# A planned attention-plus-MLP kernel: new planner rules, longer stretches, and another string of rules

## The chip, the cores and the metric

The kernel runs on one core of a Trainium2 chip. The metric is the device time of one execution, in microseconds (us). A core has five engines with instruction streams of their own, which meet at semaphores: TensorE (PE in the profile; PEld is its weight loads), VectorE (DVE), ScalarE (ACT), GpSimd (POOL) and SyncE (SP), which issues transfers. TensorE writes into PSUM, eight banks of 128 partitions by 512 float32 columns. The other engines read PSUM and write to SBUF.

## What is computed

One block on a sequence of 2048 rows of width 640. The input is normalized; 32 heads of width 20 attend to one shared key and value head; a dense layer with silu (width 1728) runs beside them; all is added to the input.

```python
x = A_x
xn = _layernorm(x, axis=-1)
return x + _A_ref(xn, A_wq, A_wk, A_wv, A_wo) + _B_ref(xn, B_w1, B_w2)
# _A_ref
scores = jnp.einsum("bhqd,bkd->bhqk", q, k) * (Dh ** -0.5)
p = _softmax(scores, axis=-1)
o = jnp.einsum("bhqk,bkd->bhqd", p, v)
# _B_ref
h = _silu(jnp.einsum("bsd,df->bsf", x, w1))
out = jnp.einsum("bsf,fd->bsd", h, w2)
```

## The kernel before

**Tiles of scores.** The queries are cut into 4 chunks of 512 rows, the heads into 8 sets of 4. A group is one chunk with one set of heads: 32 groups. In each group there are 16 blocks of 128 keys and 4 heads, so 64 tiles of 128 keys by 512 queries, 2048 in all. Each tile is one matmul of contraction 32 (`s_mm`, L1078). Four heads sit in four row groups of the array, so up to four such matmuls run at once: a *score burst*.

**Two ways to the exponential.** A tile goes one of two ways.

- By ScalarE: two or three tiles in neighbouring banks are read by one `Exp` instruction (L1166) and written to a ring of 20 slots in SBUF. When the four heads of a key block are there, one *value pass* (four column matmuls, L1201, kind `p`) multiplies them by the values and adds into a PSUM bank of the group.
- By VectorE: four tiles of one key block are turned, one after the other (the first pass, L1409), into 16-bit integers that are the bits of a rough power of two. Two shifted copies of the four tiles are made by VectorE (L1453) or GpSimd (L1448), and three value passes (kind `pd`) use the three versions with fixed weights, so that the errors of the rough power cancel in the sum.

`claim` picks the key blocks that go by VectorE, `make_s_act` the tiles that go by ScalarE, as the planner comes to them. The division is thus an outcome of the planning.

**Other work of TensorE.** Projections of queries and the dense layer run as sets of four column matmuls (L447; some, cut by rows, ride in free row groups of score bursts: L454). They fill the time between score bursts. Changing between score bursts (row tiles) and the sets of column matmuls is called a turn here.

**Who sets the order.** All instruction streams are written by a planner on the host, before the program is built (`build`, class `Sched`). It keeps a clock for each engine with costs in nanoseconds for each operation, and takes, step by step, the operation that comes next on the engine that is furthest behind. On TensorE `step_pe` does this: it lists what could run, each with a kind (`s` score burst for ScalarE, `d` a tile for VectorE, `p` and `pd` the two kinds of value passes, `m` and `l` other matmuls, `r` a row piece of one), keeps those that are ready within 40 ns, and takes the first by a list of kinds. Which list depends on the array's mode and on how far the value passes lag behind the exponentials:

```python
        order = ["s", "m0"]
        if mode == "s":
            order += ["d", "r"]
            order += ["p", "pd", "m", "l"] if lag >= ru.lagmax else ["m", "pd", "p", "l"]
```

If nothing is ready for a while, `filler` puts in a matmul of zeros (L1725). The numbers that steer all this (`ru.lagmax`, `ru.open`, `ru.need` and so on) come from `BASE`. They are altered for stretches of planned time: a string `PLAN` holds one letter for each stretch of `PIECE` nanoseconds, and a letter names a set of changed numbers in `RULES`. Past the end of the string the letter is "a", which changes nothing.

```python
        if sc.t["pe"] >= piece * PIECE:
            ru.__dict__.update(BASE)
            ru.__dict__.update(RULES[rule(piece)])
            piece += 1
```

`emit` then turns the planned order into streams with semaphore waits. On the chip each engine follows its stream in order.

**The end.** When the last group's value passes are done, ScalarE copies the bank to SBUF (L1302), TensorE adds up the softmax denominators (L999), VectorE takes reciprocals (L1002), TensorE spreads them (L1017), VectorE multiplies (L1026), and the last projections (L447) are stored (L967, L984). The dense layer's last products, in sets of 320 columns, are put where the planner finds room.

Of the kernel before, what the change touches and what calls it, by code (L numbers as in the profile page):

```python
# [14 lines left out]
P = 128  # L15
D = 640
H = 32
# [64 lines left out]
POOL_J = (2,)  # L82
SWITCH = {"s": 97.0, "p": 98.0, "f": 98.0}
SPRIO = 0.5
PIECE = 10000.0
STEPS = 1
YC = (0, 0, 3, 3)
EARLY = 1
# [13 lines left out]
ACT_LN = (5, 7)  # L102
TRACT = (0, 1)

BASE = dict(uopen=4, umin=3, uleft=3, uwait=500.0, pace=-1.0, lagl=3, half=6, hold2=0, bnd=4, pj=6000.0, rows=0, rowmin=3, lagmax=6, lagp=0, lagj=6, openlag=5, late=-0.02, lead=0.01, leadmax=0.02, need=640.0, hold=300.0, dwant=600.0, slack=700.0, dnow=400.0, hungry=0.0, patience=0.0, keep=460.0, open=2, zcap=9, stay=0.0, homes=1, want=1, claim=6)
RULES = dict(a={}, b=dict(keep=0.0), c=dict(lagp=3), d=dict(lagp=5), e=dict(lagp=0), f=dict(patience=200.0), g=dict(dwant=0.0),
             h=dict(zcap=4), i=dict(zcap=3), j=dict(homes=0), k=dict(leadmax=-1.0, lead=-1.0), l=dict(lead=0.08, leadmax=0.1),
             m=dict(need=740.0), n=dict(hold=0.0), o=dict(stay=640.0), p=dict(open=1), q=dict(slack=560.0), r=dict(hungry=1000.0), s=dict(claim=9), t=dict(open=3), u=dict(claim=4), v=dict(want=2), w=dict(slack=850.0), x=dict(hold2=4), y=dict(bnd=0), z=dict(pj=-1e9), A=dict(rows=0), B=dict(rows=2, rowmin=2), C=dict(pj=2000.0), D=dict(openlag=3), E=dict(pj=8000.0), F=dict(hold2=3), G=dict(rows=1), H=dict(half=0), I=dict(half=3), J=dict(stay=560.0), K=dict(stay=720.0), P=dict(need=560.0), Q=dict(hold=120.0), L=dict(uopen=3), M=dict(uopen=4), N=dict(uopen=5), O=dict(uopen=0))
PLAN = "acbgxnoQpQJvpnaQodtxzpvEoQJBJoaodpJqQaDqJovpkBrnvxBxQJBfaaooHoatano"


def rule(n):
    return PLAN[n] if n < len(PLAN) else "a"
PACE = 1.0
# [214 lines left out]
def build(nc, A_x, A_wq, A_wk, A_wv, A_wo, B_x, B_w1, B_w2, out, stack):  # L329
    S = A_x.shape[1]  # L330
    F = B_w1.shape[1]
# [86 lines left out]
    R = {}  # L418
# [613 lines left out]

    ru = SimpleNamespace(**BASE)
    att = {"sgroup": 0, "pgroup": 0, "n": 0, "items": 0, "value": 0.0, "lead": 0.0}
# [327 lines left out]
    def dve_items():  # L1362

        busy = sc.pe_set[1] if sc.pe_set is not None and sc.t["pe"] <= sc.pe_set[2] + 1.0 else frozenset()
        pick = None
        if cur_job[0] is not None and cur_job[0].job.rest:
            need = {r for v in cur_job[0].job.rest.values() for r in v}
            if len(need - busy) == 1:
                pick = next(((st, j) for st in open_b for j in st["left"] if j not in busy and j not in need), None)
        if pick is None:  # L1370
            pick = next(((st, j) for st in open_b for j in st["left"] if j not in busy), None)
        if pick is None and len(open_b) < ru.open:
            c = claim()
            if c is not None:
                g, kt = c
                st = {"g": g, "kt": kt, "zi": z_slot(), "left": list(range(HG)), "p1": [], "pv": None, "jobs": {}}
                batches.append(st)
                z_last[st["zi"]] = st
                open_b.append(st)
                pick = next(((st, j) for j in st["left"] if j not in busy), None)  # L1380
        if pick is None and open_b:
            pick = open_b[0], open_b[0]["left"][0]
        if pick is None:
            return None
        st, i = pick
        if i not in st["jobs"]:
            st["jobs"][i] = dve_job(st, i)
        return st["jobs"][i]
# [431 lines left out]
    def xbank_est(mode):  # L1820
        return min(bank_at(b, mode) for b in xbanks())

    def dve_idle(t):
        for op in sc.pools["dve"]:
            e = sc.est(op)
            if e is not None and e < t:
                return False
        return True
# [13 lines left out]
    def step_pe():  # L1842
        t = sc.t["pe"]
        mode = sc.pe_mode
        rd = []
        late = None
        s_at = None
        for op, kind, what in pe_candidates():
            e = sc.est(op)
            if e is None:  # L1850
                continue
            if what[0] == "pv":
                if fresh_u():
                    e = max(e, xbank_est(op.mode))
                else:
                    e = max([e] + [o.fin + sc.way(o, op) for o in sc.hazards_of(sc.banks[ubank[what[1]]]) if o.eng != "pe"])
            if what[0] in ("new", "dj"):
                if what[0] == "dj" or (what[1][0].job.bank is None and what[1][0].job.fixed is None):
                    e = max(e, xbank_est(op.mode))
            if kind == "d" and not sc.joined(op) and not (sc.t["dve"] < t + ru.hungry and dve_idle(t + ru.hungry)):  # L1860
                continue
            if kind == "s":
                rest = sc.free.difference(op.run)
                if not pro and rest:
                    dj = dve_items()
                    if dj is not None:
                        for tb in sorted(bank_at(b, "s") for b in rest)[:ru.want]:
                            if e < tb <= act_until(att["n"]) - ru.slack:
                                e = tb
                s_at = e  # L1870
                if ru.keep and mode == "f" and cur_job[0] is not None and t + 250.0 < act_until(att["n"]) - ru.keep:
                    e = max(e, t + 240.0)
            if e <= t + 40:
                rd.append((kind, op, e, what))
            elif late is None or e < late[0]:
                late = (e, op, what)
        lag = lag_now()
# [4 lines that stand above are left out]
        elif mode == "p":  # L1882
            order += ["p", "pd", "m", "d", "l"] if lag >= (ru.lagj if cur_job[0] is not None else ru.lagl if att["lead"] < ru.pace else ru.lagp) else ["m", "pd", "p", "d", "l"]
        else:
            order += ["p", "m", "pd", "d", "l"] if lag >= ru.lagmax + 1 else ["m", "l", "pd", "p", "d"]
        if mode != "s" and sc.t["dve"] < t + ru.dnow and dve_idle(t + ru.dnow):
            order.remove("d")
            order.insert(2, "d")
        if ru.stay and mode != "s" and not pro and t + 230.0 < act_until(att["n"]) - ru.stay:
            order.remove("s")  # L1890
            order.insert(len(order) - 1, "s")
        if all(not u for u in unclaimed) and not make_s_act():
            order = ["p", "pd", "d", "r", "m0", "m", "l", "s"]
        order += ["z", "x"]
        if ru.bnd and att["pgroup"] < NGR and pv_left[att["pgroup"]] <= ru.bnd and not pro:
            order = [k for k in order if k not in ("m", "l")] + [k for k in order if k in ("m", "l")]
        best = None
        for kind, op, e, what in rd:
            if kind not in order:
                continue  # L1900
            k = order.index(kind)
            if best is None or k < best[0]:
                best = (k, op, e, what)
        if best is not None:
            op = best[1]
            if op.mode != mode and s_at is not None and s_at - t < WAITS and op.mode != "s":
                return s_at, None, None
            return best[2], op, best[3]
        gap = 999.0 if late is None else late[0] - t
        if gap > (FILLGAP if mode != "p" or not att["n"] else FILLGAP2) and (streamed() < FILL or not att["n"]) and (pro or misc or make_s_act()):  # L1910
            op = filler(gap)
            e = sc.est(op) if op is not None else None
            if e is not None and e <= t + 40:
                return e, op, ("fill", None)
        if late is None:
            return None
        return late[0], late[1], late[2]

    def fresh_u():
        return att["pgroup"] < NGR and att["pgroup"] not in ubank  # L1920
# [63 lines left out]
    while not finished():  # L1984
# [3 lines that stand above are left out]
# [186 lines left out]
```

## Time and profile before

| | |
|---|---|
| median of 3 runs | 689.98 us (689.96 to 690.01) |
| profiled execution | 690.16 us |
| its span, first to last instruction | 688.3 us |
| TensorE busy | 675.7 us (98%) |
| ScalarE busy | 666.4 us (97%) |
| VectorE busy | 591.3 us (86%) |
| GpSimd busy | 581.7 us (85%) |
| granted TensorE clock | 1.0 |

A row of a group names the line, the engine, the operation, what is written and read, the shape and the count; behind the bar stand the busy time, the mean length of one and the idle time ahead of them, with what ended it. A row of the order in time has the start, the length, and the same names; several equal instructions in a row are one line. Matmuls overlap: the length of one is from issue to its modelled end, so the distance between starts tells what one costs its engine. The same holds for ScalarE, whose records overlap a little.

### The profile page before, as it was taken

To read this page: it belongs to the slowest core of one execution; us is meant where nothing else is said; L and a number is where in the kernel's file an instruction comes from. 1 tells how busy PE (TensorE), PEld (TensorE's weight loads), DVE (VectorE), ACT (ScalarE), POOL (GpSimd) and SP (SyncE) were. 2 spreads that over 40 slices of the span, in tenths; PEclk is the share of its full clock that TensorE was granted. 3 is DMA by queue.
4 is the path that set the end of the run, shared out by engine and by line. 5 is a ranking of instruction groups with operands and counts; after the bars stand their busy time and mean duration, and the time that the engine had idled before them with its cause. 6 is when DMAs were issued, how large, how long until landed. Compare 5 with 4: busy or idle time off the path is not lost.

```text
span 688.3 us, 22511 instructions
## 1 busy us (share of the span) xinstructions
PE 675.7 (98%) x9821; PEld 232.2 (34%) x9821; DVE 591.3 (86%) x1017; ACT 666.4 (97%) x728; POOL 581.7 (85%) x349
## 2 busy tenths in 40 slices
PE   8999999999999999999999999999999999999998
PEld 6432222222333333322323333332233333333345
DVE  7899988999989878798898897889999898987953
ACT  6999999999999999999999999999999999999992
POOL 6658899898988998899898889888889987879990
PEclk9999999999999999999999999999999999999999
DMA  8643220222221222422022222132222221223201
GB/s 226 190 160 42 19 23 14 35 34 25 23 29 12 32 38 29 72 36 30 9 22 30 29 31 33 26 37 61 31 22 20 21 27 23 32 20 70 23 7 41
DMA packets 34241, 28.97 MB, mean 42 GB/s; under 512 B 15486, under 2 KB 29662, under 8 KB 34142
## 3 DMA queue, kind: packets, MB, share of 16 engines
q1 hardware_dynamic: 33854, 27.20, 25.8%
q8 instruction: 77, 1.26, 0.8%
q10 hardware_dynamic: 288, 0.33, 0.1%
q14 instruction: 22, 0.18, 0.1%
HBM read 11.09 MB, written 2.62 MB: 20 GB/s over the span
## 4 chain that ended last, share of the span: by engine, by line
ACT 52%; PE 42%; DVE 3%; POOL 1%; DMA 0%; issue 0%; DVEq 0%; ACTq 0%
ACT sbt L1166 48%; PE psall L1201 14%; PE psall L1078 14%; PE psall L447 13%; ACT sbt L773 3%; DVE sbt L1409 2%; POOL sbt L1448 1%; PE psall L595 1%; PE psall L621 1%; DVE sbt L1453 0%; DMA sbt<-in_A_x_dram 0%; PE psall L999 0%; PE psall L1017 0%; ACT sbt L554 0%; DVE sbt L565 0%
## 5 line engine op out<-in xcount | busy, mean ns | idle before, releaser
L1166 ACT ACTIVATE sbt<-psall 128x1024 bf16<-128x1024 f32 (+1 forms) x656 | 640.0, 1138 | 3.2 <-PE psall L1078 3.0
L1448 POOL TENSOR_SCALAR sbt<-sbt 128x2048 int16<-128x2048 int16 x273 | 518.6, 1900 | 72.5 <-PE psall L1201 15.3
L1409 DVE TENSOR_SCALAR sbt<-psall 128x512 int16<-128x512 f32 x676 | 440.1, 685 | 63.1 <-PE psall L1078 58.0
L1078 PE MATMUL psall<-sbt 32*128 32x512 bf16 x2048 | 268.3, 384 | 3.3 <-ACT sbt L1166 2.0
L1201 PE MATMUL psall<-sbt 128*32 128x512 bf16 x3400 | 264.7, 384 | 1.9 <-POOL sbt L1448 0.6
L447 PE MATMUL psall<-sbt 128*32 128x320 bf16 (+2 forms) x3772 | 225.9, 332 | 2.1 <-DVE sbt L776 0.7
L1078 PEld LDWEIGHTS psall<-sbt 32*128 32x128 bf16 x2048 | 71.8, 91 | 236.9 <-ACT sbt L1166 174.1
L447 PEld LDWEIGHTS psall<-sbt 128*32 128x32 bf16 x3772 | 80.4, 95 | 85.5 <-issue 45.4
L1201 PEld LDWEIGHTS psall<-sbt 128*32 128x32 bf16 x3400 | 68.8, 94 | 115.5 <-issue 71.9
L1453 DVE TENSOR_SCALAR sbt<-sbt 128x2048 int16<-128x2048 int16 x65 | 47.6, 750 | 0.0
L860 POOL TENSOR_TENSOR sbt<-sbt 128x512 bf16<-128x512 f32 x30 | 38.3, 1277 | 4.9 <-DVE sbt L1453 2.7
L776 DVE SCALAR_TENSOR_TENSOR sbt<-sbt,psall 128x512 bf16<-128x512 bf16 x52 | 35.5, 682 | 3.8 <-ACT sbt L773 1.8
L773 ACT ACTIVATE sbt<-psall 128x512 bf16<-128x512 f32 x52 | 34.9, 671 | 0.2 <-PE psall L447 0.2
L454 PE MATMUL psall<-sbt 32*128 32x320 bf16 (+1 forms) x78 | 24.4, 313 | 0.0
L1250 DVE COPY sbt<-psall 128x512 f32<-128x512 f32 x31 | 21.2, 683 | 0.9 <-PE psall L1201 0.8
L919 DVE SCALAR_TENSOR_TENSOR sbt<-psall,sbt 128x320 f32<-128x320 f32 x8 | 3.9, 491 | 12.2 <-PE psall L447 7.0
L903 DVE SCALAR_TENSOR_TENSOR sbt<-psall,sbt 128x320 bf16<-128x320 f32 x24 | 11.6, 482 | 3.1 <-PE psall L447 1.7
L693 DVE TENSOR_SCALAR sbt<-psall 128x512 bf16<-128x512 f32 x20 | 13.5, 676 | 0.0
L572 POOL TENSOR_TENSOR sbt<-sbt 128x2 f32<-128x2 f32 x8 | 5.7, 710 | 8.5 <-DVE sbt L570 8.2
L1725 PE MATMUL psall<-sbt 128*32 128x256 bf16 (+1 forms) x188 | 11.1, 375 | 1.2 <-DVE sbt L487 1.2
L585 POOL TENSOR_SCALAR sbt<-sbt 128x640 bf16<-128x640 bf16 x12 | 10.4, 878 | 1.5 <-DVE sbt L577 1.5
L563 DVE BATCH_NORM_STATS2 sbt<-sbt 128x6 f32<-128x320 bf16 x14 | 6.6, 472 | 2.0 <-DMA sbt<-in_A_x_dram 2.0
(64 smaller groups left out, 118.3 us busy)
## 6 DMA issues: line engine op xcount, KB each, us to landing
sbt<-sbt SPq DMA_DIRECT2D x120, 64.0 KB, 3.8
sbt<-in_A_x_dram SPq DMA_DIRECT2D x28, 160.0 KB, 3.9
sbt<-sbt SPq DMA_DIRECT2D x213, 20.0 KB
out_dram<-sbt SPq DMA_DIRECT2D x14, 160.0 KB, 2.2
sbt<-in_B_w_dram SPq DMA_DIRECT2D x1, 2160.0 KB, 11.5
sbt<-in_B_w_dram SPq DMA_DIRECT2D x1, 2080.0 KB, 8.2
sbt<-sbt SPq DMA_DIRECT2D x75, 8.0 KB
sbt<-in_A_wq_dram SPq DMA_DIRECT2D x1, 800.0 KB, 6.7
```

The source lines that it names most:

```text
L447: ins = pe.matmul(ps[j * SLOT:(j + 1) * SLOT, b * BANK + off:b * BANK + off + n], w[:, j * SLOT:(j + 1) * SLOT], x, start=start, stop=stop ...
L454: return pe.matmul(ps[0:w.shape[-1], b * BANK:b * BANK + n], w[k], x[k], start=start, stop=stop, tile_position=(r * SLOT, 0))
L773: t = Op("act", lambda a: a.activation(t_buf[0:rows, ts, :], bk(job.bank, 0, QW, rows=rows), AF.Tanh, scale=0.5), t_act(512), ACT_END, pre ...
L776: u = Op("dve", lambda v: v.scalar_tensor_tensor(out=hT[par][0:rows, fk, :], in0=t_buf[0:rows, ts, :], scalar=1.0, in1=bk(job.bank, 0, QW, ...
L860: nm = pool(lambda e: e.tensor_tensor(oU[:, us, :], U_sb[:, us, :], Rrep, ALU.mult), 1356.0, POOL_END, pre=[uc] + lc + pack_op.get(divmod( ...
L1078: return pe.matmul(bk(b), kT_rep[i * SLOT:(i + 1) * SLOT, kt * P:(kt + 1) * P], qT[i * SLOT:(i + 1) * SLOT, g % NQ, :], start=True, stop=T ...
L1166: return a.activation(Ebuf[:, es * QW:es * QW + w], ps[:, buf[0] * BANK:buf[0] * BANK + w], AF.Exp, scale=ESCALE)
L1201: ins = pe.matmul(ps[i * SLOT:(i + 1) * SLOT, ub * BANK:ub * BANK + QW], lhsT, rhs, start=(first and k < HG), stop=(last and k >= len(lst) ...
L1250: return v.tensor_copy(U_sb[:, us, :], bk(ub))
L1409: p1 = Op("dve", lambda v: v.tensor_scalar(z16[:, i * QW:(i + 1) * QW], bk(job.bank), ZBIAS, 0.0, ALU.add, ALU.max), t_dve(QW) + 2.0, DVE_ ...
L1448: op = pool(lambda v, t=t, j=j, zin=zin: v.tensor_scalar(t.bitcast(I16), zin, float(SHIFT[j]), 1.0, ALU.add, ALU.mult), POOL_SHIFT, POOL_E ...
L1453: op = dve(lambda v, t=t, j=j, zin=zin: v.tensor_scalar_add(t.bitcast(I16), zin, float(SHIFT[j])), t_dve(N, 4), prio=SPRIO - 0.01 * j, **args)
```

## The change

- `BASE` gets a new number `pdf`, 0 unless a rule sets it. In `step_pe`, when it is 1, the kind `pd` (value passes of VectorE's tiles) is put just ahead of `p` (those of ScalarE's); when it is 2, into second place of the list.
- `RULES` gets three letters: R (`pdf` 1), S (`pdf` 2), T (`pdf` 1 and `lagp` 3).
- `PIECE` goes from 10 to 16 us of planned time.
- `PLAN` is another string, of 42 letters in place of 67. R is at three places of it (the thirteenth, fourteenth and twenty-third stretch), S and T at none.

The rest of the text of the kernel is the same. What TensorE, and behind it the other engines, do in which order follows from the string.

```diff
-PIECE = 10000.0
+PIECE = 16000.0
...
-BASE = dict(uopen=4, umin=3,
+BASE = dict(pdf=0, uopen=4, umin=3,
...
+ R=dict(pdf=1), S=dict(pdf=2), T=dict(pdf=1, lagp=3))
-PLAN = "acbgxnoQpQJvpnaQodtxzpvEoQJBJoaodpJqQaDqJovpkBrnvxBxQJBfaaooHoatano"
+PLAN = "apQdxxjnrnvQRRnomBoamCRqhJPJahEzraJBnBBGQF"
...
         if all(not u for u in unclaimed) and not make_s_act():
             order = ["p", "pd", "d", "r", "m0", "m", "l", "s"]
+        if ru.pdf and "pd" in order:
+            order.remove("pd")
+            order.insert(order.index("p") if ru.pdf == 1 else 1, "pd")
         order += ["z", "x"]
```

More of the change, by code (lines that the diff above doesn't have):

```diff
@@ L103 @@
 TRACT = (0, 1)
-BASE = dict(uopen=4, umin=3, uleft=3, uwait=500.0, pace=-1.0, lagl=3, half=6, hold2=0, bnd=4, pj=6000.0, rows=0, rowmin=3, lagmax=6, lagp=0, lagj=6, openlag=5, late=-0.02, lead=0.01, leadmax=0.02, need=640.0, hold=300.0, dwant=600.0, slack=700.0, dnow=400.0, hungry=0.0, patience=0.0, keep=460.0, open=2, zcap=9, stay=0.0, homes=1, want=1, claim=6)
+BASE = dict(pdf=0, uopen=4, umin=3, uleft=3, uwait=500.0, pace=-1.0, lagl=3, half=6, hold2=0, bnd=4, pj=6000.0, rows=0, rowmin=3, lagmax=6, lagp=0, lagj=6, openlag=5, late=-0.02, lead=0.01, leadmax=0.02, need=640.0, hold=300.0, dwant=600.0, slack=700.0, dnow=400.0, hungry=0.0, patience=0.0, keep=460.0, open=2, zcap=9, stay=0.0, homes=1, want=1, claim=6)
 RULES = dict(a={}, b=dict(keep=0.0), c=dict(lagp=3), d=dict(lagp=5), e=dict(lagp=0), f=dict(patience=200.0), g=dict(dwant=0.0),
              h=dict(zcap=4), i=dict(zcap=3), j=dict(homes=0), k=dict(leadmax=-1.0, lead=-1.0), l=dict(lead=0.08, leadmax=0.1),
-             m=dict(need=740.0), n=dict(hold=0.0), o=dict(stay=640.0), p=dict(open=1), q=dict(slack=560.0), r=dict(hungry=1000.0), s=dict(claim=9), t=dict(open=3), u=dict(claim=4), v=dict(want=2), w=dict(slack=850.0), x=dict(hold2=4), y=dict(bnd=0), z=dict(pj=-1e9), A=dict(rows=0), B=dict(rows=2, rowmin=2), C=dict(pj=2000.0), D=dict(openlag=3), E=dict(pj=8000.0), F=dict(hold2=3), G=dict(rows=1), H=dict(half=0), I=dict(half=3), J=dict(stay=560.0), K=dict(stay=720.0), P=dict(need=560.0), Q=dict(hold=120.0), L=dict(uopen=3), M=dict(uopen=4), N=dict(uopen=5), O=dict(uopen=0))
-PLAN = "acbgxnoQpQJvpnaQodtxzpvEoQJBJoaodpJqQaDqJovpkBrnvxBxQJBfaaooHoatano"
+             m=dict(need=740.0), n=dict(hold=0.0), o=dict(stay=640.0), p=dict(open=1), q=dict(slack=560.0), r=dict(hungry=1000.0), s=dict(claim=9), t=dict(open=3), u=dict(claim=4), v=dict(want=2), w=dict(slack=850.0), x=dict(hold2=4), y=dict(bnd=0), z=dict(pj=-1e9), A=dict(rows=0), B=dict(rows=2, rowmin=2), C=dict(pj=2000.0), D=dict(openlag=3), E=dict(pj=8000.0), F=dict(hold2=3), G=dict(rows=1), H=dict(half=0), I=dict(half=3), J=dict(stay=560.0), K=dict(stay=720.0), P=dict(need=560.0), Q=dict(hold=120.0), L=dict(uopen=3), M=dict(uopen=4), N=dict(uopen=5), O=dict(uopen=0), R=dict(pdf=1), S=dict(pdf=2), T=dict(pdf=1, lagp=3))
+PLAN = "apQdxxjnrnvQRRnomBoamCRqhJPJahEzraJBnBBGQF"
 def rule(n):
```

## The prediction

> **What bounds the kernel now.** I read the page's busy shares, then the groups by shape, then the order in time of ScalarE, then its end.
>
> ```profile
> span 688.3 us, 22511 instructions
> PE 675.7 (98%) x9821; PEld 232.2 (34%) x9821; DVE 591.3 (86%) x1017; ACT 666.4 (97%) x728; POOL 581.7 (85%) x349
> ACT 52%; PE 42%; DVE 3%; POOL 1%; DMA 0%; issue 0%; DVEq 0%; ACTq 0%
> ```
> ```profile
> L1166 ACT ACTIVATE sbt<-psall 128x1024 bf16<-128x1024 f32 x594 | 563.5, 1100 | 2.6 <-PE psall L1078 2.5
> L1166 ACT ACTIVATE sbt<-psall 128x1536 bf16<-128x1536 f32 x61 | 89.7, 1512 | 0.6 <-PE psall L1078 0.6
> L1166 ACT ACTIVATE sbt<-psall 128x512 bf16<-128x512 f32 x1 | 0.7, 700 | 0.0
> L773 ACT ACTIVATE sbt<-psall 128x512 bf16<-128x512 f32 x52 | 34.9, 671 | 0.2 <-PE psall L447 0.2
> ```
> ```profile
> 13.64 1.92 ACT L1166 ACTIVATE sbt<-psall 128x1024 bf16<-128x1024 f32 x2
> ...
> 22.62 7.44 ACT L1166 ACTIVATE sbt<-psall 128x1024 bf16<-128x1024 f32 x8 [0.48 <-PE psall L1078]
> 29.87 0.68 ACT L631 ACTIVATE sbt<-psall 128x512 bf16<-128x512 f32 x1
> ...
> 48.97 0.77 ACT L773 ACTIVATE sbt<-psall 128x512 bf16<-128x512 f32 x1
> 49.44 5.82 ACT L1166 ACTIVATE sbt<-psall 128x1024 bf16<-128x1024 f32 x6
> ...
> 671.73 1.54 ACT L1166 ACTIVATE sbt<-psall 128x1536 bf16<-128x1536 f32 x1
> 673.07 1.54 ACT L1166 ACTIVATE sbt<-psall 128x1536 bf16<-128x1536 f32 x1
> 674.40 0.70 ACT L1166 ACTIVATE sbt<-psall 128x512 bf16<-128x512 f32 x1
> ```
>
> TensorE and ScalarE are both nearly full, so the share does not decide. ScalarE's records overlap their neighbours, so I price it by the distance from start to start: eight exponentials of two tiles (a tile is 512 columns) take 29.87 - 22.62 = 7.25 us, 0.906 each; one of three tiles 674.40 - 673.07 = 1.33; a tanh of one tile 49.44 - 48.97 = 0.47. Between the first exponential (13.64) and the end of the last (675.10) lie 661.5 us. Work at those prices is 594 x 0.906 + 61 x 1.33 + 0.7 for the single tile + 52 x 0.47 + about 2.4 for five other tile-wide reads (kT and the paired tanh) = 647. So about 14 us of 661 are late starts, and the rest is ScalarE running without a pause: it is the bound, and its tiles are the currency. Ahead of it lies a prologue of 13.64 us, behind it a tail of 688.3 - 675.1 = 13.2 us.
>
> TensorE's pieces, in its order of time:
>
> ```profile
> 301.02 0.39 PE L1078 MATMUL psall<-sbt 32*128 32x512 bf16 x3
> 301.34 0.62 PE L447 MATMUL psall<-sbt 128*32 128x512 bf16 x8
> 301.89 0.39 PE L1078 MATMUL psall<-sbt 32*128 32x512 bf16 x3
> ```
> A score burst costs 0.32 to the next instruction, two sets of four column matmuls 0.55 with the turn back to scores, so a set is 0.22 and a turn about 0.1. One burst with two sets is 0.87, just under ScalarE's 0.906; one with three is 1.09, above it. That is where late starts come from.
>
> **The change part by part.** The edits that can be read off the diff cost nothing at run time: a longer stretch, new letters and a new string are host code that orders the instructions. R (value passes of VectorE's tiles ahead of ScalarE's) stands at three of 42 places of the string, S and T at none. What matters is the order that comes out. I compared the built programs instruction by instruction. Up to about 37 us (the first twenty-odd exponentials) the order is the same but for one projection matmul that moves past a burst, so the prologue stays. Behind it everything is rearranged.
>
> 1. *Division of tiles.* VectorE makes 672 first passes (L1409) in place of 676, so ScalarE gets four tiles more: 587 exponentials of two tiles and 67 of three against 594 and 61, and again one single. That is -7 x 0.906 + 6 x 1.33 = **+1.66 us**, on the path. A tile is 1.33 - 0.906 = 0.42, so the fixed part of an instruction is about 0.906 - 0.85 = 0.06, and having one fewer returns little. The Trainium skill (Perfetto Trace Analysis, section Optimizing Scalar/DVE Operations) says that grouping into larger operations raises throughput on a saturated engine, and gives about 51 ns of overhead for ScalarE on PSUM: by that rule alone the change would gain 0.05 us. The trace agrees with the size, and four more tiles outweigh it.
>
> ```profile
> L1448 POOL TENSOR_SCALAR sbt<-sbt 128x2048 int16<-128x2048 int16 x273 | 518.6, 1900 | 72.5 <-PE psall L1201 15.3
> L1409 DVE TENSOR_SCALAR sbt<-psall 128x512 int16<-128x512 f32 x676 | 440.1, 685 | 63.1 <-PE psall L1078 58.0
> L1453 DVE TENSOR_SCALAR sbt<-sbt 128x2048 int16<-128x2048 int16 x65 | 47.6, 750 | 0.0
> ```
> 2. *Other engines.* VectorE loses four first passes, two of four additions of partial sums (L1249) and six of 65 shifts (L1453); GpSimd gets four shifts more (277 for 273, 1.9 us each). At 86% and 85% busy both can take it: nothing, as long as TensorE does not come to a value pass ahead of its shift. If that cover fails, each miss stops TensorE, and all that is queued behind the pass, for up to one 1.9 us shift. The SP queue issues the same 520 transfers, at other places among the work.
>
> 3. *Score bursts that wait for the exponential just before.* An exponential can be fed in time if its banks were last used two exponentials back. By the banks in the two programs, three exponentials of before use banks of their direct predecessor: one in the prologue, which stays, and these two, which are gone.
>
> ```profile
> 251.47 1.08 ACT L1166 ACTIVATE sbt<-psall 128x1024 bf16<-128x1024 f32 x1
> 253.15 1.45 ACT L1166 ACTIVATE sbt<-psall 128x1536 bf16<-128x1536 f32 x1 [0.60 <-PE psall L1078]
> ...
> 512.40 1.06 ACT L1166 ACTIVATE sbt<-psall 128x1024 bf16<-128x1024 f32 x1
> 513.64 0.60 ACT L773 ACTIVATE sbt<-psall 128x512 bf16<-128x512 f32 x1 [0.18 <-PE psall L447]
> ```
> They cost 253.15 - 251.47 - 0.906 = 0.77 and 513.64 - 512.40 - 0.906 = 0.33: **-1.1 us**. A third stall, at the memset of L1533 (0.54 idle ahead of the exponential at 543.41), has its counterpart in the new order and stays.
>
> 4. *Overfull windows.* I added TensorE's prices between each two bursts that feed ScalarE. Windows over the running exponential by 0.2 to 0.4 us: four before (one is the wait at 253 above), fourteen after, for instance three value sets with a filler behind, or five half-width sets. Of the other three before, one shows a pause:
>
> ```profile
> 653.20 1.45 ACT L1166 ACTIVATE sbt<-psall 128x1536 bf16<-128x1536 f32 x1
> 654.95 1.02 ACT L1166 ACTIVATE sbt<-psall 128x1024 bf16<-128x1024 f32 x1 [0.30 <-PE psall L1078]
> ```
> 0.30 in three is 0.1 each. Eleven more, at bounds of 0 (a short window ahead pays for it) and 0.30: 0 to 3.3; I take 0.1 each, **+1.1 us**.
>
> 5. *The tail.*
>
> ```profile
> 673.97 1.41 PE L447 MATMUL psall<-sbt 128*32 128x320 bf16 x36
> 675.20 0.39 PE L1201 MATMUL psall<-sbt 128*32 128x512 bf16 x4
> 675.42 2.62 PE L447 MATMUL psall<-sbt 128*32 128x320 bf16 x72
> 677.97 1.05 PE L999 MATMUL psall<-sbt 128*128 128x4 f32 x8
> 678.95 1.08 PE L1017 MATMUL psall<-sbt 128*32 128x128 f32 x32
> 679.85 1.34 PE L447 MATMUL psall<-sbt 128*32 128x128 bf16 x44
> ```
> After the last value pass (675.20, right behind the last exponential) TensorE runs without a pause to the last products. Eighteen half-width sets (72 matmuls, 2.55 us, 0.14 each) lie there now, all ahead of the sums (L999). In the new order there are nine ahead of the sums and seventeen behind the spread (L1017), 26 in all: 8 x 0.14 = **+1.1 us**. The nine still cover the copies that the sums wait for, so that wait does not come out. The last value pass itself stays tied to the last exponential; the shift ahead of it on GpSimd could add up to 1 us.
>
> 6. *Fillers* (L1725, zero matmuls where TensorE would stand idle).
>
> ```profile
> L1725 PE MATMUL psall<-sbt 128*32 128x512 bf16 x32 | 2.8, 384 | 0.0
> L1725 PE MATMUL psall<-sbt 128*32 128x256 bf16 x156 | 8.5, 373 | 1.2 <-DVE sbt L487 1.2
> ```
> Full-width ones go from 8 sets to 22, half-width ones from 39 to 44. Where they fill idle time they cost 0; where the burst behind was ready, 0.22 and 0.11 each: 0 to 3.6 us. I take 0, since an idle TensorE under a busy ScalarE is the case in which they are placed, and keep the upper end.
>
> Sum: 1.66 - 1.1 + 1.1 + 1.1 = +2.8 on the profiled execution's 690.16 (span 688.3 and 1.9 around it), 692.9. That execution is 0.18 above the median of the runs, 689.98, so the forecast is **692.7 us** (+0.4%).
>
> **The rivals.**
>
> *Faster: TensorE's slack takes the late starts away.* Between feeding bursts TensorE has 26 ns less than ScalarE per exponential before, 34 after: over 655 exponentials 17 and 22 us. If late starts shrink with the slack, by 17/22, the 14 us lose 3.2, and the overfull windows then cost nothing: 692.7 - 3.2 - 1.1 = 688.4. It decides once late starts fall by over 2.8 us without the windows' share. For it: with more slack a late burst is made up for sooner. Against: windows of the kind 1.09 for 0.906, over by 0.1 to 0.2 us, are nearly as many as before, 96 for 102 in the two programs.
>
> *No change: TensorE is the bound.* By busy share it leads, 98% to 97%. Its work without fillers stays: two value sets and one burst fewer, two projection sets and one half-width set more, and 1,267 turns between scores and columns for 1,272, at 0.1 each -0.5 us. With the tail's +1.1 the median is 689.98 + 0.6 = 690.6. Against it: ScalarE shows 14 us of late starts in 661, while TensorE at 0.87 per usual burst waits for ScalarE:
>
> ```profile
> PEld psall L1078 <- ACT sbt L1166: 174.1, 486, 1.0
> ```
> The Trainium skill (TensorEngine Tiling (Array Packing), section Key Properties) says that changing the tiling mode drains TensorE; the turn of 0.1 us in the rows agrees, and by that rule five turns fewer speak for the change.
>
> *Slower still: the fillers are in the way.* All of part 6 at its upper end: 692.7 + 3.6 = 696.3. For it: the planner foresaw more gaps, which is also a sign of value passes that come late. Against: where a burst has to wait for ScalarE anyway, a filler ahead of it is free, and the row above has 486 such waits.
>
> **How the numbers follow.** Slower as summed 0.48, with a range of its own from 691.4 (windows free) to 694.9 (windows at 0.30); fillers 0.16; no change 0.22; faster 0.14. Within 0.2% (1.4 us) a measurement of this kernel can hardly tell a change, so slower has 0.48 + 0.16 = 0.64, same 0.22, faster 0.14. The range leaves out most of the faster rival and reaches to the filler one: 689.2 to 696.3.
>
> **What would show it.** Right: 587 and 67 exponentials at the same spacings; no pause of 0.6 at a bank of the direct predecessor; ScalarE's last exponential ending 1 to 3 us later than 675.1; some 14.3 us from there to the end, with 17 half-width sets behind L1017. Wrong: the last exponential ending at or ahead of 675 (the slack was worth more than the tiles), or TensorE waiting on L1448 or L1453 for several us in the stretches with R (192 to 224 and 352 to 368 us in the planner's time).

## The result, and the profile after

The changed kernel takes 691.84 us (median of 14 runs, 691.27 to 692.43) against 689.98 for the kernel before (median of 14 runs beside it, 689.70 to 690.82; the three shown ahead have the same median): ratio 1.0027, with a 95% interval of 1.002 to 1.0034. Run again later, beside the kernel before, it took 691.99 against 689.64, ratio 1.0032 [1.0019, 1.0046]. It is slower by some 2 us, 0.3%.

The page of the changed kernel: span, busy time of each engine, and the shares of the chain that ended last.

```profile
span 689.5 us, 22651 instructions
PE 676.7 (98%) x9897; PEld 234.3 (34%) x9897; DVE 585.9 (85%) x1005; ACT 667.3 (97%) x727; POOL 588.6 (85%) x353
ACT 53%; PE 41%; POOL 3%; DVE 2%; issue 1%; DMA 0%; ACTq 0%
```

Its groups by shape (count, busy time, mean of one, idle time ahead):

```profile
L1166 ACT ACTIVATE sbt<-psall 128x1024 bf16<-128x1024 f32 x587 | 560.8, 1107 | 2.5 <-PE psall L1078 2.4
L1166 ACT ACTIVATE sbt<-psall 128x1536 bf16<-128x1536 f32 x67 | 99.6, 1515 | 0.1
...
L1409 DVE TENSOR_SCALAR sbt<-psall 128x512 int16<-128x512 f32 x672 | 437.6, 683 | 72.3 <-PE psall L1078 68.5
L1453 DVE TENSOR_SCALAR sbt<-sbt 128x2048 int16<-128x2048 int16 x59 | 44.7, 771 | 2.7 <-PE psall L1201 2.6
```

The counts are the forecast ones: 587 and 67 exponentials, 672 first passes, 59 shifts on VectorE. Shares and means hardly move, so they don't say where the time went. The order in time at the end does: first ScalarE, then TensorE.

```profile
667.75 7.41 ACT L1166 ACTIVATE sbt<-psall 128x1536 bf16<-128x1536 f32 x6
675.75 0.66 ACT L1302 ACTIVATE sbt<-psall 128x256 f32<-128x256 f32 x2 [0.59 <-PE psall L1201]
```
```profile
675.31 0.39 PE L1201 MATMUL psall<-sbt 128*32 128x512 bf16 x4
675.52 1.40 PE L447 MATMUL psall<-sbt 128*32 128x320 bf16 x36
676.85 1.05 PE L999 MATMUL psall<-sbt 128*128 128x4 f32 x8
677.84 1.08 PE L1017 MATMUL psall<-sbt 128*32 128x128 f32 x32
678.73 7.42 PE L447 MATMUL psall<-sbt 128*32 128x320 bf16 x212
```

The last exponential ends at 667.75 + 7.41 = 675.16, where before it ended at 675.10. From there to the end it is 14.3 us for 13.2. So in the profiled executions (691.27 for 690.16) the whole +1.1 us lies behind the last exponential. The two are not typical: 691.27 is the fastest of the changed kernel's runs, and 690.16 is among the slower ones of the kernel before.

The 661.6 us ahead of it hold two changes that cancel. Work at the prices of the prediction (start to start, 0.904 for two tiles here) is 587 x 0.904 + 67 x 1.33 + 52 x 0.477 + 2.4 = 646.95, which is 1.65 more than before. Late starts, each distance from start to start less that price, add up to 13.9 us for 15.5, which is 1.6 less. ScalarE has more to do, and loses as much less to late starts.

### The profile page after: what moved, and what is told of

It is laid out like the page before. It is cut to its first block, busy times and chain, and to the rows that moved or that the text cites. A ratio compares the mean times of both kernels' runs of the same rounds, so it can differ in the third digit from the quotient of the medians.

```text
span 689.5 us, 22651 instructions
## 1 busy us (share of the span) xinstructions
PE 676.7 (98%) x9897; PEld 234.3 (34%) x9897; DVE 585.9 (85%) x1005; ACT 667.3 (97%) x727; POOL 588.6 (85%) x353
## 3 DMA queue, kind: packets, MB, share of 16 engines
q8 instruction: 77, 1.26, 0.7%
## 4 chain that ended last, share of the span: by engine, by line
ACT 53%; PE 41%; POOL 3%; DVE 2%; issue 1%; DMA 0%; ACTq 0%
ACT sbt L1166 49%; PE psall L1201 14%; PE psall L1078 13%; PE psall L447 11%; ACT sbt L773 3%; POOL sbt L1448 2%; DVE sbt L1409 1%; PE psall L595 1%; PE psall L621 1%; PE psall L1725 1%; DMA sbt<-in_A_x_dram 0%; PE psall L1017 0%; PE psall L999 0%; DVE sbt L1453 0%; ACT sbt L554 0%
## 5 line engine op out<-in xcount | busy, mean ns | idle before, releaser
L1448 POOL TENSOR_SCALAR sbt<-sbt 128x2048 int16<-128x2048 int16 x277 | 526.2, 1900 | 66.6 <-DVE sbt L1453 27.3
L447 PE MATMUL psall<-sbt 128*32 128x320 bf16 (+2 forms) x3784 | 223.7, 332 | 1.3 <-DVE sbt L1409 0.7
L447 PEld LDWEIGHTS psall<-sbt 128*32 128x32 bf16 x3784 | 81.9, 95 | 80.8 <-issue 42.5
L1453 DVE TENSOR_SCALAR sbt<-sbt 128x2048 int16<-128x2048 int16 x59 | 44.7, 771 | 2.7 <-PE psall L1201 2.6
L860 POOL TENSOR_TENSOR sbt<-sbt 128x512 bf16<-128x512 f32 x30 | 38.3, 1277 | 7.3 <-DVE sbt L1453 4.5
L776 DVE SCALAR_TENSOR_TENSOR sbt<-sbt,psall 128x512 bf16<-128x512 bf16 x52 | 35.5, 682 | 5.0 <-PE psall L1201 1.7
L773 ACT ACTIVATE sbt<-psall 128x512 bf16<-128x512 f32 x52 | 36.4, 701 | 0.0
L454 PE MATMUL psall<-sbt 32*128 32x320 bf16 x74 | 22.5, 305 | 0.0
L1250 DVE COPY sbt<-psall 128x512 f32<-128x512 f32 x31 | 21.1, 681 | 1.1 <-PE psall L1201 1.0
L1725 PE MATMUL psall<-sbt 128*32 128x256 bf16 (+1 forms) x264 | 15.6, 340 | 1.2 <-DVE sbt L487 1.2
L595 PE MATMUL psall<-sbt 128*128 128x128 bf16 x80 | 7.0, 220 | 1.7 <-DVE sbt L588 1.7
```

The lines of the kernel that those rows point to most:

```text
L447: ins = pe.matmul(ps[j * SLOT:(j + 1) * SLOT, b * BANK + off:b * BANK + off + n], w[:, j * SLOT:(j + 1) * SLOT], x, start=start, stop=stop ...
L454: return pe.matmul(ps[0:w.shape[-1], b * BANK:b * BANK + n], w[k], x[k], start=start, stop=stop, tile_position=(r * SLOT, 0))
L773: t = Op("act", lambda a: a.activation(t_buf[0:rows, ts, :], bk(job.bank, 0, QW, rows=rows), AF.Tanh, scale=0.5), t_act(512), ACT_END, pre ...
L776: u = Op("dve", lambda v: v.scalar_tensor_tensor(out=hT[par][0:rows, fk, :], in0=t_buf[0:rows, ts, :], scalar=1.0, in1=bk(job.bank, 0, QW, ...
L860: nm = pool(lambda e: e.tensor_tensor(oU[:, us, :], U_sb[:, us, :], Rrep, ALU.mult), 1356.0, POOL_END, pre=[uc] + lc + pack_op.get(divmod( ...
L1448: op = pool(lambda v, t=t, j=j, zin=zin: v.tensor_scalar(t.bitcast(I16), zin, float(SHIFT[j]), 1.0, ALU.add, ALU.mult), POOL_SHIFT, POOL_E ...
```

## Experiments

All edits are to the changed kernel unless said otherwise. The runs come from three chips; the kernel before takes 689.64, 689.74 and 689.71 us on them. The changed kernel was run beside it on the first only, 691.99 us, and the experiments on single windows are read against that. Between chips a difference of 0.1 us thus says nothing.

### The changed kernel once more

> The changed kernel once more, for a second profile beside the first. Both theories expect some 1.8 us more than before. The question is the spread: fourteen runs of the changed kernel lie 1.2 us apart, thirteen of fourteen runs of before only 0.4. If the spread is in one place (the score burst that waits for the memset of L1533 on GpSimd, 0.94 us late in the first profile), this place differs between the two profiles by several tenths of a microsecond; if it is spread over many late starts, no single place differs by more than 0.2.

691.99 us (691.38 to 692.28). Its profile (span 689.6) has no place that differs from the first by over 0.3 us, the memset's included. That does not settle where the spread comes from, as both profiled executions, 691.27 and 691.38, are the fastest of their runs.

### Fillers of eight columns

```diff
+        m = 8 if att["n"] > 4 else n
-   pe.matmul(ps[..., ub * BANK:ub * BANK + n], ..., zero_t[:, 0:n],
+   pe.matmul(ps[..., ub * BANK:ub * BANK + m], ..., zero_t[:, 0:m],
```

> The changed kernel with its order as it is, but every filler behind the prologue only 8 columns wide instead of 512 or 256 (27 sets, about 5 us of TensorE's work less). Theory (ScalarE is the bound, fillers lie in idle time): the time of the changed kernel within 0.5 us. Rival (fillers stand in the way of ready bursts): up to 3.6 us and more faster than the changed kernel. Rival (TensorE is the bound): about 5 us faster. A danger for the reading: a granted clock below 1.0, which would make it slower.

691.72 us, ratio 1.0036 [1.0021, 1.005], a span of 689.9. The trace has 124 matmuls of eight columns, 31 sets, where the expectation counted 27. Cutting most of the fillers' time behind the prologue returned nothing that can be told from the changed kernel. They lie in time that TensorE has to spare; the fillers' rival falls, and so does the plainest form of "TensorE is the bound".

### Eight half-width sets fewer in the tail

```diff
+    end = max(i for i, op in enumerate(pe) if op.name.startswith("spread"))
+    out = [op for op in pe[end:] if op.name.startswith("y") and op not in needed and op.ends == (False, False)][:8]
...
+                if op in out:
+                    pass
```

> The changed kernel without eight of the seventeen half-width sets behind the spread (L1017) at the end; a part of the dense layer's last product is left out. Theory (behind the last exponential TensorE runs without a pause, each set is on the path): 8 x 0.135 = 1.1 us faster than the changed kernel. Rival (the sets lie beside VectorE's multiplication L1026 and cost nothing): the same time as the changed kernel.

690.55 us (690.09 to 691.81), 1.4 below the changed kernel; the span is 688.3, which is 1.3 below the 689.6 beside it. TensorE's order in time at its end:

```profile
677.76 1.08 PE L1017 MATMUL psall<-sbt 128*32 128x128 f32 x32
678.65 6.33 PE L447 MATMUL psall<-sbt 128*32 128x320 bf16 x180
```

32 matmuls fewer (180 for 212) shorten the row by 7.42 - 6.33 = 1.09 us, 0.136 a set. The tail's term is confirmed in place and in size.

### Sixteen exponentials cut by a tile

```diff
+            if n in (93, 135, 146, 201, 217, 230, 252, 283, 319, 364, 379, 402, 419, 445, 511, 587):
+                cut = 2 * QW
```

> The changed kernel, its order as it is, but sixteen of its 67 three-tile exponentials, spread between 93 and 587, read two tiles only; the third tile of each is left out. Theory (ScalarE's tiles are the currency): 16 x 0.426 = 6.8 us faster than the changed kernel, less some tenths for windows in which TensorE then is behind; between 4 and 6.8 us. Rival (TensorE is the bound): less than 1 us.

691.60 us, ratio 1.0029 [1.0018, 1.004]: 0.4 us returned for 6.8 us of work taken off ScalarE. ScalarE's work at the prices above falls to 640.1, and its late starts rise from 13.9 to 21.1. Behind every one of the sixteen cuts they grow by 0.29 to 0.43 us within the next dozen exponentials, 6.4 us in all. Another 1.1 stand at two places without a cut, where a value pass waits for a shift of GpSimd (0.63 at 77 us and 0.49 at 478 us, a place that comes back below), and 0.3 is saved elsewhere; this profiled execution, 692.10, is the slowest of its runs. One place shows how. Here the exponential at 465.08 reads two tiles, while in the changed kernel (464.50) it reads three. ScalarE of the cut kernel (its line is L1171 there), from two stretches of the order in time:

```profile
465.99 0.78 ACT L773 ACTIVATE sbt<-psall 128x512 bf16<-128x512 f32 x1
466.46 2.13 ACT L1171 ACTIVATE sbt<-psall 128x1024 bf16<-128x1024 f32 x2
...
468.71 1.02 ACT L1171 ACTIVATE sbt<-psall 128x1024 bf16<-128x1024 f32 x1
```

Two exponentials from 466.46 should make room for the third at 466.46 + 2 x 0.904 = 468.27; it starts at 468.71, 0.44 late, which is the tile that was cut. TensorE of the changed kernel, and then of the cut one (value passes are L1206 there), over the same stretch between two score bursts:

```profile
466.16 0.39 PE L1078 MATMUL psall<-sbt 32*128 32x512 bf16 x3
466.48 1.26 PE L1201 MATMUL psall<-sbt 128*32 128x512 bf16 x20
467.68 0.40 PE L1078 MATMUL psall<-sbt 32*128 32x512 bf16 x4
```
```profile
466.76 0.39 PE L1078 MATMUL psall<-sbt 32*128 32x512 bf16 x3
467.08 1.26 PE L1206 MATMUL psall<-sbt 128*32 128x512 bf16 x20
468.28 0.40 PE L1078 MATMUL psall<-sbt 32*128 32x512 bf16 x4
```

Both take 1.52 us from burst to burst, with five value sets and no pause between. In the changed kernel the lead that the first burst has over its exponential covers this long window. With ScalarE 0.43 further on, the lead is used up, and TensorE sets the pace. The chain that ended last tells the same of the whole execution:

```profile
PE 70%; ACT 17%; POOL 5%; DVE 5%; issue 1%; DMA 1%; SPq 0%; DVEq 0%; POOLq 0%
```

ScalarE has 17% of it, for 53% in the changed kernel. (The 53% moves easily: the second execution of the same kernel has 34%. The late starts are the firmer evidence.) That ScalarE's tiles are the currency of the time is refuted for single tiles, a few among many windows.

### Column sets made narrow in the same windows

```diff
+class Thin:
+    def matmul(self, out, w, x, **kw):
+        return self.pe.matmul(out[:, 0:64], w, x[:, 0:64], **kw)
...
+        got = [op for op in pe[at[f"S{n}"] + 1:at[f"S{n + 2}"]] if op in later][:2]
+        for op in got:
+            op.fn = lambda e, fn=op.fn: fn(Thin(e))
```

> The changed kernel, its order as it is, with two sets of column matmuls behind each of the sixteen score bursts of the run with shorter exponentials made 64 columns wide instead of 512 or 320 (32 sets, about 0.15 to 0.19 us each, 5 to 6 us of TensorE's work; that part of the sums is left out). Theory A (ScalarE is the bound): the changed kernel's time within 0.5 us. Theory B (TensorE is the bound, which the run with the shorter exponentials allows): 4 to 6 us faster. Theory C (the plan fits the two to each other window by window, and neither has slack): within 1 us.

692.04 us, ratio 1.0031 [1.002, 1.0042]: nothing returned. TensorE is not the bound either, at least not in the windows where ScalarE has its longest instructions.

### Both cuts at once

> The two cuts together: the sixteen exponentials with two tiles in place of three, and the 32 narrow sets of TensorE in the same windows. Theory A: 5 to 6.8 us faster than the changed kernel, as the shorter exponentials alone should have been and were not. Theory B: no more than with the narrow sets alone. Theory C: 4 to 6 us faster, although each cut alone gives less than 1 us.

690.80 us, ratio 1.0018 [1.0008, 1.0028]: about 1.2 us returned, and span 688.8. That is more than the two alone (0.4 and 0), and far from what either cut took away. None of the three theories forecast it: A and C wanted 4 us and more, B nothing. Exponential by exponential against the changed kernel, starts jump ahead by 0.1 to 0.45 us behind most of the cuts, and much of it is given back within the next two exponentials. At the window shown above the two bursts are 1.61 us apart here, with the same five value sets: the narrow sets lie ahead of them and not between, so TensorE sets the pace there again (0.07 of the 1.61 is a wait for a shift ahead of the fifth set). Within a dozen exponentials of the cuts 5.8 of the 6.8 us are given back. The largest single step back stands apart from them: the exponential at 477.68 is 0.68 later than its place in the order, because a value pass waits for a shift of GpSimd behind the multiply described below. Why the other windows give back what both engines saved was not followed; it stays open.

### Score bursts that don't wait for the memset

```diff
+        a = pool(lambda g: g.memset(qT[:, 2, :], 0.0), ..., name="selz")
...
+            if op.eng == "pe" and op.mode == "s":
+                op.deps = {d for d in op.deps if d.name != "selz"}
```

This is the third stall of the prediction's part 3. The memset clears one of ten slots of the query buffer, one that no later score burst reads; the planner ties them together through the zero rows that it books once for all slots. In the changed kernel it looks so (GpSimd, TensorE, ScalarE in order of time):

```profile
549.63 0.95 POOL L1533 MEMSET sbt<- 128x512 bf16 x1
550.73 0.40 PE L1078 MATMUL psall<-sbt 32*128 32x512 bf16 x3 [0.88 <-POOL sbt L1533]
551.15 1.96 ACT L1166 ACTIVATE sbt<-psall 128x1024 bf16<-128x1024 f32 x2 [0.76 <-PE psall L1078]
```

> The changed kernel with the score bursts no longer waiting for the memset of L1533, which clears a part of the query tile that no later score burst reads (the planner saw a dependence through the zero rows, which all groups share). The order is the same. Theory: this place holds up TensorE and ScalarE together (0.94 us late in the profile), so the time falls by 0.6 to 0.9 us. Rival: the burst is late for another reason, the end of the exponential ahead, and the time stays.

690.99 us (690.34 to 691.65), ratio 1.0017 [1.0008, 1.0026]: 1.0 us below the changed kernel, of which 0.94 comes at this place. ScalarE, without the wait, runs through:

```profile
544.61 9.46 ACT L1166 ACTIVATE sbt<-psall 128x1024 bf16<-128x1024 f32 x10
```

### The same release in the kernel before

> The kernel before with its own instructions in its own order; its score bursts alone no longer wait for the memset of L1533, which writes other rows than they read. Theory (the stall of 0.54 us ahead of the exponential at 543 us, 0.69 over its usual distance, is on the path, since nothing behind it pays it back): -0.5 to -0.7 us, 689.0 to 689.3, faster than both kernels. Rival (the time is given back within some ten exponentials, as the cuts of single windows were): -0.2 to 0, 689.5 to 689.8.

689.66 us, ratio 1.0 [0.9992, 1.0009]: nothing, as the rival had it, though not spread over ten exponentials. The pause at 543 us is gone, and another stands 8 us behind it. GpSimd, TensorE and ScalarE of this kernel in order of time:

```profile
543.27 9.82 POOL L1448 TENSOR_SCALAR sbt<-sbt 128x2048 int16<-128x2048 int16 x5
...
551.17 0.40 PE L1201 MATMUL psall<-sbt 128*32 128x512 bf16 x4 [0.70 <-POOL sbt L1448]
551.50 0.39 PE L1078 MATMUL psall<-sbt 32*128 32x512 bf16 x4
...
551.93 1.94 ACT L1166 ACTIVATE sbt<-psall 128x1024 bf16<-128x1024 f32 x2 [0.73 <-PE psall L1078]
```

and the same burst in the kernel before, without that wait:

```profile
543.27 9.81 POOL L1448 TENSOR_SCALAR sbt<-sbt 128x2048 int16<-128x2048 int16 x5
```
```profile
551.49 0.43 PE L1078 MATMUL psall<-sbt 32*128 32x512 bf16 x4
```

GpSimd's run of five shifts starts at 543.27 in both. TensorE, 0.7 us earlier, comes to a value pass whose shift is not ready, and issues the burst behind it at 551.50 for 551.49. The same edit is worth 0.94 us where the next resource has slack, and nothing where it has none.

### GpSimd's multiply behind the shifts

Several profiled executions, of kernels with an edit elsewhere, differ from the changed kernel's at this one place by half a microsecond and more. GpSimd's normalization multiply (L860) at 472 us waits for four transfers (L856); two shifts stand behind it in its queue. GpSimd of the changed kernel, and then of the run with narrow column sets, each with the transfers on SP's queue:

```profile
464.84 3.40 SPq L856 DMA_DIRECT2D sbt<-sbt  x4
471.88 1.28 POOL L860 TENSOR_TENSOR sbt<-sbt 128x512 bf16<-128x512 f32 x1 [0.64 <-DVE sbt L1453]
473.25 3.88 POOL L1448 TENSOR_SCALAR sbt<-sbt 128x2048 int16<-128x2048 int16 x2
```
```profile
465.40 3.72 SPq L856 DMA_DIRECT2D sbt<-sbt  x4
472.80 1.28 POOL L860 TENSOR_TENSOR sbt<-sbt 128x512 bf16<-128x512 f32 x1 [1.76 <-DVE sbt L776]
...
476.11 0.40 PE L1201 MATMUL psall<-sbt 128*32 128x512 bf16 x4 [0.46 <-POOL sbt L1448]
478.09 0.40 PE L1201 MATMUL psall<-sbt 128*32 128x512 bf16 x4 [0.49 <-POOL sbt L1448]
479.07 2.85 ACT L1166 ACTIVATE sbt<-psall 128x1024 bf16<-128x1024 f32 x3 [0.69 <-PE psall L1078]
```

With the transfers issued half a microsecond later the multiply starts 0.92 later, two value passes wait for shifts, and ScalarE loses 1.0 us against its price. The rows of the multiply name instructions of VectorE, but in the second trace L776 ends at 472.25, half a microsecond earlier; the last of the four transfers lands at 471.76 in the first and at 472.67 in the second, 0.13 ahead of the multiply in both.

```diff
+    at = [i for i, op in enumerate(pool) if op.occ == 1356.0][20]
+    pool.insert(at + 2, pool.pop(at))
```

> The changed kernel with one instruction moved on GpSimd alone: the normalization multiply (L860) at 472 us stands behind the next shift of its queue (L1448) instead of ahead of it. Theory (the multiply waits in order for transfers, the shifts queued behind it come late in some executions, and that costs 0.3 to 1.0 us there): the median falls by 0.3 to 0.8 us against the changed kernel, to 691.0 to 691.6, and no late exponential of over 0.4 us stands between 470 and 481 us. Rival (the spread comes from elsewhere, the wait only shows it): 691.7 to 692.1, as the changed kernel, with the late starts at another place.

The multiply comes behind both shifts, as the rows below show, one more than the expectation says. 691.36 us (691.18 to 691.88), ratio 1.0024 [1.0015, 1.0034]: 0.6 below the changed kernel. The fastest execution is where it was (691.18 for 691.27), those above 691.9 are gone. This profile happens to hold late transfers, and they cost nothing:

```profile
465.39 3.91 SPq L856 DMA_DIRECT2D sbt<-sbt  x4
471.98 3.88 POOL L1448 TENSOR_SCALAR sbt<-sbt 128x2048 int16<-128x2048 int16 x2 [0.70 <-DVE sbt L1453]
475.94 1.27 POOL L860 TENSOR_TENSOR sbt<-sbt 128x512 bf16<-128x512 f32 x1
```

### The string without R, and the longer stretches alone

```diff
-PLAN = "apQdxxjnrnvQRRnomBoamCRqhJPJahEzraJBnBBGQF"
+PLAN = "apQdxxjnrnvQaanomBoamCaqhJPJahEzraJBnBBGQF"
```

> The changed kernel with its string, in which the three letters R are replaced by a, so that the new rule never acts. The planner then makes another order from the first R on: 539 exponentials of two tiles and 110 of three (1408 tiles for ScalarE instead of 1376), and hardly any half-width set is left behind the last score burst (3 instead of 34). If the division of tiles sets the time: 13.3 us more of ScalarE's work and some 2 to 3 us less tail, so about 10 to 11 us slower than the changed kernel. If TensorE's work sets it, which is nearly the same: within 3 us of the changed kernel.

710.36 us, ratio 1.0298 [1.0277, 1.0319]: 18.4 above the changed kernel, where the division of tiles alone was to give 10 to 11. The second is the kernel before with its own string:

```diff
-PIECE = 10000.0
+PIECE = 16000.0
```

> The longer stretches alone: the kernel before with PIECE 16000 and its old string. The planned order then has 513 exponentials of two tiles and 134 of three in place of 594 and 61, and the planner ends 26 us later. Theory A (a string fits only the stretches that it was searched for; VectorE makes fewer tiles and ScalarE takes them over): ScalarE's work is +73 x 1.33 - 81 x 0.904 = +23.9 us, 710 to 718. Theory B (the stretch is a small matter, the string does not hang on it): within 3 us of the kernel before, 687 to 693.

716.98 us, ratio 1.0395 [1.0376, 1.0414], as theory A had it. The groups by shape, without R and then with the longer stretches alone:

```profile
L1166 ACT ACTIVATE sbt<-psall 128x1024 bf16<-128x1024 f32 x539 | 521.4, 1107 | 4.8 <-PE psall L1078 4.7
L1166 ACT ACTIVATE sbt<-psall 128x1536 bf16<-128x1536 f32 x110 | 163.9, 1551 | 4.1 <-PE psall L1078 4.1
```
```profile
L1166 ACT ACTIVATE sbt<-psall 128x1024 bf16<-128x1024 f32 x513 | 499.2, 1111 | 2.9 <-PE psall L1078 2.6
L1166 ACT ACTIVATE sbt<-psall 128x1536 bf16<-128x1536 f32 x134 | 201.7, 1555 | 5.1 <-PE psall L1078 5.1
```

Of the +18.2 us of span without R, +12.9 is ScalarE's work, +7.2 late starts and -2.3 the tail. Of the +27.3 with longer stretches, +22.5 is work, +7.2 late starts, -3.2 the tail. The rest, in both, is the last exponential's length. Here ScalarE's tiles make the larger part of the difference, since dozens of them move. The late starts are not taken apart: the whole order is another, and the granted clock fell to 0.97 or 0.98 in two stretches of 100 us of each run, which the changed kernel's profile does not show. On this evidence a string fits the stretches and rules that it was made for, and neither part of the change can be judged without the others.

### Three letters of the old string exchanged, with the release

```diff
-PLAN = "acbgxnoQpQJvpnaQodtxzpvEoQJBJoaodpJqQaDqJovpkBrnvxBxQJBfaaooHoatano"
+PLAN = "acbgxnoQpQJvpnaQodtxzpvEoQJBJoaodpJqQaDqJovpkBrnvxBxQJBfaaooHoaKSnk"
```

> The kernel before with the same release from the memset of L1533, with the old stretches of 10 us, and with three letters near the end of the old string exchanged (the last five are KSnk behind oa instead of atano; S is one of the new rules). The planner ends its own clock 0.30 us earlier for that string than for the old one. Theory (differences of the planner's clock come out on the chip at about their size, as +1.83 planned and +1.9 measured did for the change): 0.2 to 0.4 us below the run with the release alone, 688.7 to 689.1. Rival (differences that small drown in when transfers land): the same as the release alone within 0.2.

689.76 us, ratio 1.0001 [0.9992, 1.001]: nothing. The planned 0.30 us did not come out; a pause of 1.14 us (1.26 against the price) that the kernel before does not have stands in its end:

```profile
661.80 15.91 ACT L1166 ACTIVATE sbt<-psall 128x1536 bf16<-128x1536 f32 x13 [1.14 <-PE psall L1078]
```

No version here beats the kernel before by more than can be measured.

## Why the prediction was right, and where its steps were not

Direction and range held: slower, 691.84 within 689.2 to 696.3 and 0.9 below the forecast 692.7. That the number came so near is partly luck. Of the forecast +2.8 the tail's 1.1 came out in full. Ahead of the last exponential, where +1.7 was forecast, only 0.05 came in the profiled execution, and a wait that the prediction put at nothing adds about 0.6 to the median. Step by step:

- *Division of tiles, +1.66.* The work came out as summed (+1.65), but "on the path" is the step that failed. Sixteen tiles taken away returned 0.4 of 6.8 us, so a few tiles are not worth 0.42 each; where windows were followed, TensorE's long windows and GpSimd's shifts stand close behind ScalarE and take over. The Trainium skill (Perfetto Trace Analysis, section Identifying the Most-Contended Engine) says to take the engine with the highest occupancy first, and to judge TensorE's headroom by other measures than its busy time, its weight loads among them. By that rule, with weight loads (34%) as the measure for TensorE, ScalarE (97%) is the one to relieve; the runs here do not agree, as relieving it by 6.8 us was worth 0.4. Only with dozens of tiles, as without R, does the work show in the time.
- *Other engines, nothing.* TensorE's matmuls wait for L1448 for 0.3 us in the changed kernel's profile. But the cover named there (a shift ready before its value pass) fails behind the multiply of 472 us in four of the profiles of edited kernels, by 0.5 to 1.0 us. This term was put too low: moving the multiply took 0.6 off the median.
- *Direct predecessors, -1.1.* Both waits are gone, and late starts fell by 1.1 there. The second was misread, though: what starts late at 513.64 is a tanh, and its row names column sets (L447), not a score burst. TensorE has seven column sets between the bursts of 511.41 and 513.60, and the exponential behind the tanh, whose banks are its predecessor's, starts at 514.13 and is not late. That was an overfull window. That the memset's stall stays held; it grew from 0.69 to 0.94.
- *Overfull windows, +1.1.* Mis-sized: by the same sums over the programs, whose windows are not listed here, the fourteen cost 0.8 us together, 0.06 each, where the three of before cost 0.7. The term measured +0.2. The pause that it was priced by (654.95, 0.42 against the price) was only in part the window's: just ahead of it, in the kernel before, a shift of VectorE (L1453, at 650.16) takes 1.57 us and a value pass waits for it, while in the run with the release, with the same order there, the shift takes 1.25 and the pause is 0.21. At the one window followed above, the burst ahead has a lead over its exponential; for the others that is not shown.
- *The tail, +1.1.* +1.15 in the trace, and taking it out gave 1.4 in the median, 1.1 of it in TensorE's row. It is the whole difference of the two profiled executions.
- *Fillers, nothing.* Held.

Forecast was a last exponential 1 to 3 us later; it came 0.05 later, close to the prediction's own sign of being wrong (at or ahead of 675), since the late starts fell by 1.6 in all (1.1 as forecast and 0.9 in small pieces, less 0.25 that the memset's stall and 0.16 that the windows grew). What made the small pieces smaller was not traced. The faster rival wanted more than 2.8 without the windows' share, and got 1.8. One sum is off: with the windows free the summed forecast is 692.7 - 1.1 = 691.6, not 691.4; nothing hangs on it.

The rival without change had the tail right and the sum of everything ahead of it at -0.5 us, near the measured +0.05: by the two profiled executions, +1.1 apart, its +0.6 is nearer than +2.8. But its reason fell in the form that it had, for neither fillers nor narrow column sets returned anything. The row put against it was misread too. It counts pauses of the weight loads, 0.36 us on average, and these are nearly as long, 0.34, ahead of bursts for which the profile shows no wait ("issue"). The matmuls themselves hardly wait for ScalarE. In the kernel before:

```profile
PEld psall L1078 <- issue: 30.8, 91, 0.5
```
```profile
PE psall L1078 <- ACT sbt L1166: 2.0, 4, 0.7
```

So TensorE had little slack of its own, which fits that work taken from one of the two alone returned next to nothing. That both cuts together returned no more than 1.2 us is not explained by it.

The median rises by 1.86 us. The tail is 1.15 of it, and the run with the multiply moved shows that the late multiply adds about 0.6. That makes 1.75. But beside the kernel before on another chip, with the multiply moved, the kernel is still 1.65 us slower (691.36 for 689.71), 0.5 more than the tail. This half microsecond stays open; the two profiles don't show it, in part because the profiled execution of the kernel before was slower than most.

## What to carry to other kernels

Where two engines are both at 97% or 98% in an order that was fitted to them, price an edit by the window it falls in, and ask of each gain which wait stands next behind it: the same release was worth 0.94 us in one order and nothing in the other. Work behind the last bounded instruction is the safe term; it came out at its full price. When an instruction that waits for transfers stands ahead of others on an in-order queue, look at several executions, for one profile can hold the good draw.

## What was unexpected in the hardware

- The same instructions in the same order at a place do not make the same time there: four transfers (L856) were issued at 464.8 to 464.9 or at about 465.4 us, and took 3.1 to 3.4 or 3.6 to 3.9 us on their queue; the multiply behind them began after 0.64 us of idle time or after 1.2 to 1.8. The late draw was profiled in edited kernels only, not in two executions of one kernel. What moves the transfers was not tried.
- The share of the chain of waits is not stable between executions of one kernel: ScalarE has 53% of it in one and 34% in the next, with no place that differs by over 0.3 us.
